# Hash attention and expert layers on one core: rounding the late heads' softmax planes straight from the exponentials

## The chip, the cores and the metric

The kernel runs on one core of a Trainium2 chip. A core has five engines that run side by side, each with an in-order queue of its own: TensorE (PE, matrix products; its weight loads are PEld), VectorE (DVE), ScalarE (ACT), GpSimd (POOL) and SyncE (SP), which issues most DMAs. They meet at semaphores. The metric is device time in microseconds (us), from the start of the program on the chip to its end; less is better.

## The reference

Four batches of eight heads, 768 positions, 64 columns. A position attends only to positions in its own hash bucket; a row without any partner gets a uniform softmax over all 768. The result of all heads is the input of a two-layer network with squared ReLU.

```python
q_bits = (np.einsum('bhsd,dk->bhsk', q, proj) > 0)      # 6 bits, k alike
mask = q_bucket[:, :, :, None] == k_bucket[:, :, None, :]
scores = scale * np.matmul(q, k.transpose(0, 1, 3, 2))
scores = np.where(mask, scores, -1000000000.0)
scores = scores - np.max(scores, axis=-1, keepdims=True)
attn = np.exp(scores)
attn = attn / (np.sum(attn, axis=-1, keepdims=True) + 1e-09)
x = np.matmul(attn, v)                  # then (3072 tokens) x 512
h = x @ w_in                            # 512 -> 2048
r = np.maximum(h, 0.0)
out = (s * (r * r) + b) @ w_out         # 2048 -> 512
```

## The kernel before

The program is written as steps (`plan.add`, `plan.any`), each with an engine or a choice of engines, an estimated cost, what it reads and writes, and a priority. `Plan.order` runs a small simulation with those costs and fixes the order of each engine's queue; where a step may run on several engines (`some`, `plan.any`), it takes the one that by the estimates is done first. On the chip the order is fixed; only the waits differ from the plan.

A slot is 256 rows of one head, two tiles of 128 rows; there are 32 x 3 = 96 slots. Heads 0 to 9 (slots 0 to 29) take the early way, in which the softmax is transposed by TensorE; `late(w)` is true for heads 10 to 31 (slots 30 to 95, 132 tiles), which write the softmax as two f16 planes and let a DMA transpose them.

The softmax of a slot is in `weights`. For each tile: two pairs of matmuls (L607, L608) make the scores, the hash mask among them, in a pair of PSUM banks (two pairs take turns); L612 (VectorE) takes the negated maximum into `st`; L613 (ScalarE) takes the exponential of scores plus that bias, with the row sum, into one of the five buffers of `eb`. For both tiles together, GpSimd marks rows without a partner from their maximum (L617 a huge addend for the sum, L618 the uniform value), and VectorE makes the inverse sum (L622, L623). Then GpSimd normalises each tile in place: exponential times inverse plus uniform value (L632). For late heads ScalarE rounds that times 2^15 to f16, the high plane (L639), VectorE makes the remainder, the low plane (L640), both into one of the two buffers of `pb`, and a DMA of SyncE transposes them into `tb` (L641). `values` multiplies the planes with the values (L678, L684 for late heads), `finish` moves the result to the network's input.

`st` holds for each slot of a ring of `NST` = 2 the maximum, the sum, its inverse and the two marks.

The expert layers (`moe`) need all heads of a batch. They have the lowest priority on TensorE and fill it between attention steps; a group of two 128-blocks has 24 matmuls of the first layer (L780 to L782) and 12 of the second (L807, with `ghb`, then with the remainder `glb`). Between the layers run L790 to L792 on ScalarE and L793, L794 on GpSimd. `decode` turns the experts' float64 weights into planes, on ScalarE, VectorE and GpSimd, during the first half.

Of the kernel before, what the change touches and what calls it, by code (L numbers as in the profile page):

```python
# [168 lines left out]
def lsh_attention_moe(ctx: ExitStack, tc, q, k, v, proj, w_in, w_out, s, b, out):  # L169
# [29 lines left out]
    def tile_(name, shape, dt=F32):  # L199
        return const.tile(shape, dt, name=name)  # L200
# [11 lines left out]
    def act(n, fn, r, w, pr, more=0.0, late_=0.0):  # L212
        plan.add(ACT, 0.21 + n / 1470.0 + more, fn, r, w, pr, late_)
# [74 lines left out]
    NST = 2  # L288
    misc = tile_("misc", [P, 8])
    st = tile_("st", [P, NST, 5, TPC])  # L290
# [44 lines left out]
    nc.vector.memset(zero, 0.0)  # L335
    nc.vector.memset(qk_sb[0:D], SCALE)
# [21 lines left out]
    def decode(u, pr):  # L358
# [23 lines left out]
        act(512, lambda: nc.scalar.activation(g, raw()[:, :, 1].bitcast(F32), AF.Copy, scale=float(2.0**-112)), rk + [("pace", u % PACE)], [gk], pr)  # L382
        act(512, lambda: nc.scalar.activation(words(0), raw()[:, :, 0].bitcast(U32), AF.Copy, scale=float(2.0**-29 * 0.9373)), [], rk, pr)
# [208 lines left out]
    def weights(i, pr):  # L592
# [4 lines left out]
        nm, z, rz, u, big_ = [st[:, y, m] for m in range(5)]  # L597
        nk, zk = [[("st", y, m, a) for a in range(TPC)] for m in range(2)]
        for a in range(TPC):
# [4 lines left out]
            for g in range(2):  # L604
# [11 lines left out]
        def missing():  # L616
            nc.gpsimd.tensor_scalar(big_, nm, -FLOOR, 1e30, ALU.is_gt, ALU.mult)  # L617
            nc.gpsimd.tensor_scalar(u, nm, -FLOOR, 1.0 / (S + EPS), ALU.is_gt, ALU.mult)  # L618
        pool(TPC, missing, nk, [("st", y, 3), ("st", y, 4)], pr, 0.7)
# [4 lines left out]
        dve(1, inverse, zk + [("st", y, 4)], [("st", y, 2)], pr, 0.32)  # L624
        for a in range(TPC):
            j = TPC * i + a
            e, ek = EB[ering(j)], EK[ering(j)]
            n, r = j % 2, tring(i)
            hi, lo, hk = pb[:, n, 0], pb[:, n, 1], EK[NE + n]

            def norm(eng, a=a, e=e):
                eng.tensor_scalar(e, e, rz[:, a:a + 1], u[:, a:a + 1], ALU.mult, ALU.add)  # L632
            ways = [(POOL, NORM, lambda norm=norm: norm(nc.gpsimd))]
            if not late(w) and not POOLN:
                ways.append((ACT, 0.93, lambda a=a, e=e: nc.scalar.activation(e, e, AF.Identity, bias=u[:, a:a + 1], scale=rz[:, a:a + 1])))
            plan.any(ways, [("st", y, 2), ("st", y, 3)], [ek], pr)
            if not late(w):
                continue
# [246 lines left out]
FIRST = 0.5  # L885
RATE = 1.0
# [11 lines left out]
POOLN = True  # L898
# [39 lines left out]
```

## Time and profile before

| | us |
|---|---|
| median of 3 runs | 966.34 (964.97 to 966.7) |
| profiled execution, its own time | 965.3 |
| its span, first to last instruction | 963.5 |
| TensorE busy in the span | 923.7 (96%) |
| VectorE, ScalarE, GpSimd busy | 600.3, 662.1, 589.5 |
| mean granted TensorE clock | 0.983 of full |

The durations used below come from the profiled execution. Busy time of an engine is the time covered by its instructions; a matmul's end is modelled, so TensorE's busy time alone does not say that it is at its peak. A wait is put down to the engine whose semaphore came last. An engine that is idle and not the bottleneck costs nothing.

### The profile page before, as it was taken

What the parts mean: (1) busy time and instruction counts of PE and PEld (TensorE: products, weight loads), DVE (VectorE), ACT (ScalarE), POOL (GpSimd) and SP (SyncE); (2) the same over time, 40 slices, a digit from 0 to 9 for tenths busy, and PEclk for the clock granted to TensorE, in tenths of its full rate; (3) what the DMA queues carried; (4) which work ended last, traced back from release to release, by engine and by line L of the source; (5) the groups of instructions that cost most, each with busy time, mean ns of one, the idle gap of its engine ahead of it and who ended that gap; (6) DMA issues with size and microseconds to landing.
All of it is one profiled execution on the core that took longest, in us unless ns stands there. A gap on an engine that the chain in (4) does not pass through costs nothing.

```text
span 963.5 us, 18096 instructions
## 1 busy us (share of the span) xinstructions
PE 923.7 (96%) x6512; PEld 732.1 (76%) x6512; DVE 600.3 (62%) x1020; ACT 662.1 (69%) x1235; POOL 589.5 (61%) x686
## 2 busy tenths in 40 slices
PE   8998779899999999999999999999999999999997
PEld 5876567677777777778787778877878888888886
DVE  6687887778788687676767677767667672000000
ACT  3787887888787667766677777777777775434342
POOL 2455654687598667566777666766767675433333
PEclk7999898999999999999999999999999999999999
DMA  4376675556898889997699798898897775101000
GB/s 116 93 191 197 181 197 161 142 158 154 219 200 179 188 199 200 206 202 155 141 191 183 163 205 170 165 200 162 177 188 152 170 132 105 55 9 37 12 22 22
DMA packets 303721, 144.44 MB, mean 150 GB/s; under 512 B 264256, under 2 KB 286784, under 8 KB 303632
## 3 DMA queue, kind: packets, MB, share of 16 engines
q1 hardware_dynamic: 298432, 126.25, 61.0%
q10 hardware_dynamic: 5200, 17.05, 5.9%
q8 instruction: 51, 0.84, 0.4%
q14 instruction: 38, 0.31, 0.1%
HBM read 51.38 MB, written 14.16 MB: 68 GB/s over the span
## 4 chain that ended last, share of the span: by engine, by line
PE 69%; DVE 9%; DMA 6%; POOL 6%; issue 5%; ACT 4%; POOLq 0%; SPq 0%; DVEq 0%; ACTq 0%
PE bank L807 21%; PE bank L780 7%; PE bank L782 7%; PE bank L781 7%; PE bank L607 6%; PE bank L608 5%; PE bank L678 4%; PE bank L672 3%; DVE st L612 3%; DMA tb<-pb 3%; PE bank L664 2%; PE bank L684 2%; POOL eb L632 2%; DMA vm<-in_v_dram 2%; PE bank L477 1%
## 5 line engine op out<-in xcount | busy, mean ns | idle before, releaser
L632 POOL TENSOR_SCALAR eb<-eb,st 128x768 f32<-128x768 f32 x176 | 201.0, 1147 | 57.3 <-DVE st L623 41.3
L807 PE MATMUL bank<-w,ghb 128*128 128x512 f32 x768 | 213.9, 407 | 0.0
L612 DVE TENSOR_REDUCE st<-bank 128x1 f32<-128x768 f32 x192 | 180.1, 951 | 54.0 <-PE bank L608 48.5
L780 PE MATMUL bank<-xc,wi 128*128 128x256 f16 x768 | 211.5, 275 | 0.0
L782 PE MATMUL bank<-xc,wi 128*128 128x256 f16 x768 | 209.3, 273 | 0.0
L781 PE MATMUL bank<-xc,wi 128*128 128x256 f16 x768 | 209.3, 273 | 0.0
L613 ACT ACTIVATE eb<-bank,st 128x768 f32<-128x768 f32 x176 | 157.4, 895 | 63.0 <-DVE st L612 29.8
L640 DVE SCALAR_TENSOR_TENSOR pb<-eb,pb 128x768 f16<-128x768 f32 x132 | 140.6, 1070 | 60.5 <-ACT pb L639 58.6
L793 POOL TENSOR_SCALAR rb<-rb,misc 128x512 f32<-128x512 f32 x96 | 79.8, 832 | 153.7 <-ACT ghb L792 137.8
L790 ACT ACTIVATE rb<-bank,dsc 128x512 f32<-128x512 f32 x95 | 65.3, 687 | 144.8 <-PE bank L782 137.4
L607 PE MATMUL bank<-ks,aq 128*128 128x384 f32 x384 | 147.2, 383 | 11.1 <-ACT eb L613 6.7
L807 PEld LDWEIGHTS bank<-w,ghb 128*128 128x128 f32 x768 | 135.4, 189 | 22.4 <-issue 1.0
L794 POOL TENSOR_TENSOR glb<-rb,ghb 128x512 fp32r<-128x512 f32 x96 | 132.7, 1383 | 5.8
L608 PE MATMUL bank<-ks,bq 76*128 76x384 f32 x384 | 132.7, 346 | 2.3 <-DMA bq<-nat 2.3
L639 ACT ACTIVATE pb<-eb 128x768 f16<-128x768 f32 x132 | 110.1, 837 | 22.5 <-DMA tb<-pb 20.6
L807 PE MATMUL bank<-w,glb 128*128 128x512 f32 x384 | 112.3, 401 | 1.3 <-POOL glb L794 1.3
L780 PEld LDWEIGHTS <-wi 128*128 128x128 f16 x768 | 74.9, 98 | 48.0 <-issue 41.5
L607 PEld LDWEIGHTS bank<-ks,aq 128*128 128x128 f32 x384 | 74.6, 194 | 29.1 <-ACT eb L613 10.6
L617 POOL TENSOR_SCALAR st<-st 128x2 f32<-128x2 f32 x96 | 43.3, 451 | 80.4 <-DVE st L612 68.0
L830 DVE COPY osb<-bank 128x256 f32<-128x256 f32 x4 | 1.5, 418 | 136.3 <-PE bank L807 135.7
L807 PEld LDWEIGHTS bank<-w,glb 128*128 128x128 f32 x384 | 70.2, 188 | 16.7 <-POOL glb L794 1.9
L782 PEld LDWEIGHTS <-wi 128*128 128x128 f16 x768 | 75.1, 98 | 8.6
(136 smaller groups left out, 1502.3 us busy)
## 6 DMA issues: line engine op xcount, KB each, us to landing
ks<-aq SPq DMA_DIRECT2D x60, 192.0 KB
raw<-in_moe_w_in_dram ACTq DMA_DIRECT2D x16, 512.0 KB
raw<-in_moe_w_out_dram ACTq DMA_DIRECT2D x16, 512.0 KB
xc<-xd SPq DMA_DIRECT2D x60, 128.0 KB
nat<-in_q_dram SPq DMA_DIRECT2D x32, 192.0 KB
nat<-in_k_dram SPq DMA_DIRECT2D x32, 192.0 KB
vm<-in_v_dram SPq DMA_DIRECT2D x32, 192.0 KB
xd<-xsb SPq DMA_DIRECT2D x48, 128.0 KB
```

The source lines that it names most:

```text
L607: nc.tensor.matmul(o, aq[:, ts], ks[0][:, cols], start=True, stop=False)
L608: nc.tensor.matmul(o, bq[0:HR, ts], ks[1][0:HR, cols], start=False, stop=True)
L612: dve(S, lambda a=a, sc=sc: nc.vector.tensor_reduce(nm[:, a:a + 1], sc, AX.XY, ALU.max, negate=True), bk, [nk[a]], pr, 0.88)
L613: act(S, lambda a=a, sc=sc, e=e: nc.scalar.activation(e.rearrange("p (g n) -> p g n", g=2), sc, AF.Exp, bias=nm[:, a:a + 1], accum_out=z[: ...
L632: eng.tensor_scalar(e, e, rz[:, a:a + 1], u[:, a:a + 1], ALU.mult, ALU.add)
L639: act(S, lambda e=e, hi=hi: nc.scalar.mul(hi, e, TOP), [ek], [hk], pr)
L640: dve(S, lambda e=e, hi=hi, lo=lo: nc.vector.scalar_tensor_tensor(lo, e, TOP, hi, ALU.mult, ALU.subtract), [ek, hk], [("lo", n)], pr, 1.0)
L780: nc.tensor.matmul(hp, w[:, 0, fs], xc[:, 0, :], start=(cc == 0), stop=False)
L781: nc.tensor.matmul(hp, w[:, 1, fs], xc[:, 0, :], start=False, stop=False)
L782: nc.tensor.matmul(hp, w[:, 0, fs], xc[:, 1, :], start=False, stop=(cc == NC_ - 1))
L794: pool(2 * CH, lambda r=r, gh=gh, gl=gl: nc.gpsimd.tensor_tensor(gl, r, f32(gh), ALU.subtract), [rk, hk], [lk], MP)
L807: nc.tensor.matmul(o, (gh, gh, gl)[z][:, ts], w[:, z % 2], start=(f == fa and z == 0), stop=(f == fz - 1 and z == 2))
```

## The change

For late heads the normalising pass is gone. The first rounding (high plane) multiplies the exponential by 2^15 over the sum, an operand read from memory for each row, on ScalarE or GpSimd (`HIWAYS`), and the remainder on VectorE does the same. A row without a partner is now treated in the exponential: one new VectorE instruction for each tile takes the maximum and the constant 1, each times "maximum small enough", as bias and scale of the exponential, so that both are 0 for such a row and each exponential is 1. The two marks on GpSimd are gone for late heads, and the inverse sum needs no addend. Early heads keep their steps. `st` becomes a ring of four with a column of ones, set once. The conversions of expert weights go through a helper that could choose an engine but is given only ScalarE (`CONV`).

```diff
-    NST = 2
+    NST = 4
-    st = tile_("st", [P, NST, 5, TPC])
+    st = tile_("st", [P, NST, 6, TPC])
...
+    nc.vector.memset(st[:, :, 1, :], 1.0)
...
-            act(S, lambda a=a, sc=sc, e=e: nc.scalar.activation(e.rearrange("p (g n) -> p g n", g=2), sc, AF.Exp, bias=nm[:, a:a + 1], accum_out=z[:, a:a + 1]),
-                bk + [nk[a]], [ek, zk[a]], pr, 0.15, 0.2)
...
+            if late(w):
+                dve(1, lambda a=a: nc.vector.scalar_tensor_tensor(st[:, y, 2:4, a], nm[:, a:a + 1].broadcast_to([P, 2]), -FLOOR, st[:, y, 0:2, a], ALU.is_le, ALU.mult), [nk[a]], [sk[a]], pr, 0.16)
+            act(S, lambda a=a, sc=sc, e=e: nc.scalar.activation(e.rearrange("p (g n) -> p g n", g=2), sc, AF.Exp, bias=st[:, y, 2, a:a + 1] if late(w) else nm[:, a:a + 1],
+                                                                scale=st[:, y, 3, a:a + 1] if late(w) else 1.0, accum_out=z[:, a:a + 1]), bk + [sk[a] if late(w) else nk[a]], [ek, zk[a]], pr, 0.15, 0.2)
+        rk = ("st", y, 5)
+        if not late(w):
...
+            return
 
         def inverse():
-            nc.vector.scalar_tensor_tensor(rz, z, EPS, big_, ALU.add, ALU.add)
+            nc.vector.tensor_scalar(rz, z, EPS, 1.0 / TOP, ALU.add, ALU.mult)
             nc.vector.reciprocal(rz, rz)
...
-            def norm(eng, a=a, e=e):
-                eng.tensor_scalar(e, e, rz[:, a:a + 1], u[:, a:a + 1], ALU.mult, ALU.add)
-            ways = [(POOL, NORM, lambda norm=norm: norm(nc.gpsimd))]
...
-            act(S, lambda e=e, hi=hi: nc.scalar.mul(hi, e, TOP), [ek], [hk], pr)
-            dve(S, lambda e=e, hi=hi, lo=lo: nc.vector.scalar_tensor_tensor(lo, e, TOP, hi, ALU.mult, ALU.subtract), [ek, hk], [("lo", n)], pr, 1.0)
+            some(S, lambda x, a=a, e=e, hi=hi: x.activation(hi, e, AF.Copy, scale=rz[:, a:a + 1]) if x is nc.scalar else x.tensor_scalar(hi, e, rz[:, a:a + 1], zero, ALU.mult, ALU.add), [ek, rk], [hk], pr, HIWAYS, NORM)
+            dve(S, lambda a=a, e=e, hi=hi, lo=lo: nc.vector.scalar_tensor_tensor(lo, e, rz[:, a:a + 1], hi, ALU.mult, ALU.subtract), [ek, hk, rk], [("lo", n)], pr, 1.0)
...
+CONV = (ACT,)
+CONVCOST = 0.95
...
-POOLN = True
+HIWAYS = (ACT, POOL)
```

## Rows read from the trace of the kernel before

**Rows 1.** By stretch: busy us (count) PE, PEld, DVE, ACT, POOL; clock; DMA share; GB/s.

```profile
0.00:240.00 240.00, 211.90 (x1634) 164.74 (x1634) 186.25 (x380) 183.58 (x398) 137.43 (x180) 0.94 0.59 160
240.00:320.00 80.00, 75.22 (x511) 58.04 (x510) 65.60 (x120) 62.91 (x116) 63.26 (x65) 1.00 0.89 196
320.00:805.00 485.00, 482.94 (x3355) 384.71 (x3354) 342.23 (x510) 350.78 (x628) 329.11 (x385) 1.00 0.87 176
805.00:963.00 158.00, 153.68 (x1019) 124.59 (x1016) 6.25 (x12) 64.78 (x96) 59.70 (x59) 1.00 0.11 32
```

**Rows 2.** Chain that ended last, at 341 and 866 us; start, us, what.

```profile
340.87 2.79 PE bank L807 x12
...
865.98 2.79 PE bank L807 x12
```

**Rows 3.** TensorE's waits from 240 to 320 us; total us, times, longest.

```profile
PE bank L678 <- DMA tb<-pb: 1.4, 1, 1.4
PE bank L607 <- ACT eb L613: 1.1, 2, 0.8
PE bank L477 <- DVE bq L480: 0.9, 1, 0.9
```

**Rows 4.** TensorE's waits from 320 to 810 us.

```profile
PE bank L607 <- DVE bq L480: 1.0, 2, 0.8
...
PE bank L607 <- ACT eb L613: 0.2, 1, 0.2
```

**Rows 5.** Waits of all engines from 320 to 810 us.

```profile
DVE pb L640 <- ACT pb L639: 52.1, 49, 3.6
...
ACT eb L613 <- DVE pb L640: 25.2, 21, 3.7
ACT pb L639 <- DMA tb<-pb: 17.0, 20, 1.8
...
ACT eb L613 <- DVE st L612: 6.9, 4, 2.3
```

**Rows 6.** Groups by line (busy us, mean ns, idle before); one line's durations min/median/max.

```profile
L632 POOL TENSOR_SCALAR eb<-eb,st 128x768 f32<-128x768 f32 x176 | 201.0, 1147 | 57.3 <-DVE st L623 41.3 <-ACT raw L383 4.3 <-ACT tb L228 4.1
L640 DVE SCALAR_TENSOR_TENSOR pb<-eb,pb 128x768 f16<-128x768 f32 x132 | 140.6, 1070 | 60.5 <-ACT pb L639 58.6 <-POOL xsb L733 1.3
L639 ACT ACTIVATE pb<-eb 128x768 f16<-128x768 f32 x132 | 110.1, 837 | 22.5 <-DMA tb<-pb 20.6 <-POOL eb L632 1.8
L791 ACT ACTIVATE rb<-rb 128x512 f32<-128x512 f32 x96 | 60.5, 630 | 1.8
L617 POOL TENSOR_SCALAR st<-st 128x2 f32<-128x2 f32 x96 | 43.3, 451 | 80.4 <-DVE st L612 68.0 <-DMA ks<-nat 4.7 <-PE bank L664 2.4
L622 DVE SCALAR_TENSOR_TENSOR st<-st 128x2 f32<-128x2 f32 x96 | 29.0, 302 | 28.4 <-ACT eb L613 14.2 <-POOL rb L793 6.0 <-POOL st L617 4.3
L419 ACT ACTIVATE wi<-raw,wsc 128x512 f16<-128x512 f32 x10 | 6.9, 722 | 0.4 <-DVE wsc L439 0.2
...
L622 DVE SCALAR_TENSOR_TENSOR st<-st x96: 143/160/1261, 22.7 to 795.6; 128x2 f32<-128x2 f32 x96
L640 DVE SCALAR_TENSOR_TENSOR pb<-eb,pb x132: 939/958/2043, 256.3 to 812.6; 128x768 f16<-128x768 f32 x132
```

**Rows 7.** In order of time, GpSimd and ScalarE at the first late tiles.

```profile
252.69 3.72 POOL L632 TENSOR_SCALAR eb<-eb,st 128x768 f32<-128x768 f32 x2 [0.32 <-DVE st L623]
...
255.47 0.84 ACT L639 ACTIVATE pb<-eb 128x768 f16<-128x768 f32 x1 [1.82 <-POOL eb L632]
```

**Rows 8.** The same in the middle of the late heads.

```profile
500.64 1.96 POOL L632 TENSOR_SCALAR eb<-eb,st 128x768 f32<-128x768 f32 x2 [0.56 <-DVE st L623]
...
512.05 0.84 ACT L639 ACTIVATE pb<-eb 128x768 f16<-128x768 f32 x1
...
520.77 0.84 ACT L639 ACTIVATE pb<-eb 128x768 f16<-128x768 f32 x1 [0.58 <-DMA tb<-pb]
```

**Rows 9.** Groups by line from 805 us to the end, TensorE.

```profile
L807 PE MATMUL bank<-w,glb 128*128 128x512 f32 x116 | 32.6, 396 | 1.3 <-POOL glb L794 1.3
```

More of the change, by code (lines that the diff above doesn't have):

```diff
@@ L381, in decode, with scaled, fn @@
             dve(1, lambda: nc.vector.tensor_reduce(wmx[:, j:j + 1], raw()[:, :, 1].bitcast(F32), AX.X, ALU.max, apply_absolute_value=True), rk, [("wx", j)], pr, 0.65)
-        act(512, lambda: nc.scalar.activation(g, raw()[:, :, 1].bitcast(F32), AF.Copy, scale=float(2.0**-112)), rk + [("pace", u % PACE)], [gk], pr)
-        act(512, lambda: nc.scalar.activation(words(0), raw()[:, :, 0].bitcast(U32), AF.Copy, scale=float(2.0**-29 * 0.9373)), [], rk, pr)
+        def scaled(out, src, by, r, w):
+            def fn(e):
+                if e is nc.scalar:
+                    e.activation(out(), src(), AF.Copy, scale=by)
+                else:
+                    e.tensor_scalar(out(), src(), by, 0.0, ALU.mult, ALU.add)
+            some(512, fn, r, w, pr, CONV, CONVCOST)
+        scaled(lambda: g, lambda: raw()[:, :, 1].bitcast(F32), float(2.0**-112), rk + [("pace", u % PACE)], [gk])
+        scaled(lambda: words(0), lambda: raw()[:, :, 0].bitcast(U32), float(2.0**-29 * 0.9373), [], rk)
         dve(512, lambda: nc.vector.scalar_tensor_tensor(words(0), gi, -2**31, words(0), ALU.bitwise_and, ALU.bitwise_or), [gk], rk, pr, 0.75)
@@ L596, in weights @@
         aq, bq, ks = AQ[x], BQ[x], KS[x]
-        nm, z, rz, u, big_ = [st[:, y, m] for m in range(5)]
-        nk, zk = [[("st", y, m, a) for a in range(TPC)] for m in range(2)]
+        nm, z, rz = [st[:, y, m] for m in (0, 4, 5)]
+        nk, sk, zk = [[("st", y, m, a) for a in range(TPC)] for m in (0, 2, 4)]
         for a in range(TPC):
@@ L612, in weights @@
             dve(S, lambda a=a, sc=sc: nc.vector.tensor_reduce(nm[:, a:a + 1], sc, AX.XY, ALU.max, negate=True), bk, [nk[a]], pr, 0.88)
-            act(S, lambda a=a, sc=sc, e=e: nc.scalar.activation(e.rearrange("p (g n) -> p g n", g=2), sc, AF.Exp, bias=nm[:, a:a + 1], accum_out=z[:, a:a + 1]),
-                bk + [nk[a]], [ek, zk[a]], pr, 0.15, 0.2)
-        def missing():
-            nc.gpsimd.tensor_scalar(big_, nm, -FLOOR, 1e30, ALU.is_gt, ALU.mult)
-            nc.gpsimd.tensor_scalar(u, nm, -FLOOR, 1.0 / (S + EPS), ALU.is_gt, ALU.mult)
@@ new lines, in weights, with missing, inverse @@
+        rk = ("st", y, 5)
+        if not late(w):
+            u, big_ = st[:, y, 2], st[:, y, 3]
+            def missing():
+                nc.gpsimd.tensor_scalar(big_, nm, -FLOOR, 1e30, ALU.is_gt, ALU.mult)
+                nc.gpsimd.tensor_scalar(u, nm, -FLOOR, 1.0 / (S + EPS), ALU.is_gt, ALU.mult)
+            pool(TPC, missing, nk, sk, pr, 0.7)
+            def inverse():
+                nc.vector.scalar_tensor_tensor(rz, z, EPS, big_, ALU.add, ALU.add)
+                nc.vector.reciprocal(rz, rz)
+            dve(1, inverse, zk + sk, [rk], pr, 0.32)
+            for a in range(TPC):
+                j = TPC * i + a
+                e, ek = EB[ering(j)], EK[ering(j)]
+                pool(S, lambda a=a, e=e: nc.gpsimd.tensor_scalar(e, e, rz[:, a:a + 1], u[:, a:a + 1], ALU.mult, ALU.add), [rk] + sk, [ek], pr, NORM)
+            return
@@ L621, in inverse @@
         def inverse():
-            nc.vector.scalar_tensor_tensor(rz, z, EPS, big_, ALU.add, ALU.add)
+            nc.vector.tensor_scalar(rz, z, EPS, 1.0 / TOP, ALU.add, ALU.mult)
             nc.vector.reciprocal(rz, rz)
-        dve(1, inverse, zk + [("st", y, 4)], [("st", y, 2)], pr, 0.32)
+        dve(1, inverse, zk, [rk], pr, 0.32)
         for a in range(TPC):
@@ L629, in weights @@
             hi, lo, hk = pb[:, n, 0], pb[:, n, 1], EK[NE + n]
-            def norm(eng, a=a, e=e):
-                eng.tensor_scalar(e, e, rz[:, a:a + 1], u[:, a:a + 1], ALU.mult, ALU.add)
-            ways = [(POOL, NORM, lambda norm=norm: norm(nc.gpsimd))]
[L634 to L638, printed above, removed]
-            act(S, lambda e=e, hi=hi: nc.scalar.mul(hi, e, TOP), [ek], [hk], pr)
-            dve(S, lambda e=e, hi=hi, lo=lo: nc.vector.scalar_tensor_tensor(lo, e, TOP, hi, ALU.mult, ALU.subtract), [ek, hk], [("lo", n)], pr, 1.0)
+            some(S, lambda x, a=a, e=e, hi=hi: x.activation(hi, e, AF.Copy, scale=rz[:, a:a + 1]) if x is nc.scalar else x.tensor_scalar(hi, e, rz[:, a:a + 1], zero, ALU.mult, ALU.add), [ek, rk], [hk], pr, HIWAYS, NORM)
+            dve(S, lambda a=a, e=e, hi=hi, lo=lo: nc.vector.scalar_tensor_tensor(lo, e, rz[:, a:a + 1], hi, ALU.mult, ALU.subtract), [ek, hk, rk], [("lo", n)], pr, 1.0)
             plan.add(SP, TCOST, lambda a=a, n=n, r=r: nc.sync.dma_start_transpose(tb[:, r, a].rearrange("p h t q -> p (h t) q"), pb[:, n].rearrange("p h n -> p (h n)")),
```

1 line of the change is left out of this document (removed).

## The prediction

> **What bounds the kernel now.** I read first the busy time by stretch [rows 1]. It cuts the run in four. Up to 240 us (heads 0 to 9, the early way) TensorE is busy 211.90 of 240 us; from 240 to 320 us, where the late heads start, 75.22 of 80; from 320 to 805 us (late heads and expert layers together) 482.94 of 485; behind 805 us only expert layers are left, and VectorE has all but stopped. A busy TensorE need not run at its peak, so I looked at the pace of one kind of matmul in the chain of waits: twelve of line 807 take 2.79 us at 341 us, in the middle of the late heads, and 2.79 us at 866 us, where nothing else competes [rows 2]. The busy time of the third stretch is thus work and not hidden waiting. What TensorE stands idle there is 485 - 482.9 = 2.1 us, in the second stretch 80 - 75.2 = 4.8 us: 6.9 us that a faster softmax could give back. The 28 us of the first stretch belong to early heads, whose arithmetic stays.
>
> The Trainium skill, page "Perfetto Trace Analysis", section "Identifying the Most-Contended Engine", tells the reader not to judge TensorE by its matmul busy share but by the share of its weight loads. By that rule 384.71 / 485 = 79% would leave a fifth of the stretch, some 100 us, to be won. The trace speaks against it here: in the last stretch, where TensorE waits for nothing, the same share is 124.59 / 158 = 79% [rows 1], so 79% is what this mix of matmuls loads when it is full.
>
> Next I read who waits for whom. In the second stretch TensorE's longest waits are 1.4 us for a transposing DMA into `tb` and 1.1 us for an exponential that frees a score bank [rows 3]. In the third they are 1.0 us and 0.2 us [rows 4]. In the third the other engines wait for one another: line 640 waits 52.1 us for line 639, exponentials wait 25.2 us for line 640 to free a buffer of `eb`, line 639 waits 17.0 us for the DMA to free a buffer of `pb` [rows 5]. That is a queue backed up from its far end.
>
> One slot shows how far. Its two normalising passes run at 500.64 us and are over at 502.6; the first rounding of the same tiles (line 639) starts at 512.05, nearly ten us later, and the next rounding into the same half of `pb` at 520.77, having waited for the DMA [rows 8]. One trip round that buffer is 520.77 - 512.05 = 8.7 us: rounding, remainder, DMA transposition. It sets the attention's pace; the normalising pass lies in front of it, in time that the tile spends waiting anyway.
>
> **The change part by part.** There are 66 late slots of two tiles: 132 tiles.
>
> Removed on GpSimd: 132 passes of line 632 at 1.147 us, 151 us, and in each of 66 slots line 617 at 0.451 us with its twin on the next line, at most 60 us [rows 6]. Where they lay: in steady state in the ten us above, so nothing there. At the start, where no `pb` buffer is taken, they are on the path: the first two late tiles are normalised at 252.69 us for 3.72 us, and ScalarE stood 1.82 us until the first was out [rows 7]; the exponential queued behind is the one that TensorE waits for. Without the pass those two waits should go: 1.1 us for the exponential and 1.4 us for the first transposes, which start up to 3.7 us sooner, together -2.5 us [rows 3]. Late next is then VectorE's preparation of the next head, 0.9 us in the same stretch, which stays.
>
> Added on VectorE: one instruction on 128x2 for each tile, between maximum and exponential: 132. No such row stands at this place; the nearest is line 622, the same operation and size: median 0.160 us, mean 0.302, worst 1.261. So 21 us by the median, 40 by the mean [rows 6]. I take the mean. It stands in VectorE's queue in front of whatever comes next and delays every exponential by 0.3 us. Its cover is ScalarE's own queue: in the third stretch ScalarE was idle for want of a maximum only 4 times, 6.9 us in all [rows 5]; 4 x 0.3 = 1.2 us of later exponentials, of which TensorE, which waited 0.2 us for them, should see next to nothing. If that cover goes, the price is up to 132 x 0.3 = 40 us on ScalarE, and TensorE sees what its two score banks don't hide.
>
> Pointer operands: on ScalarE a 512-wide pass with a scale read from memory takes 0.722 us (line 419) against 0.630 without (line 791), so +0.09 us for each exponential and each rounding that stays there [rows 6]: at most 132 x 2 x 0.09 = 24 us, about what a third of the roundings moved away (44 x 0.837 = 37 us) repays. For the remainder on VectorE no row isolates a pointer; I bound it between 0 and ScalarE's 0.09 us and take 0.09, 12 us. It can be less than nothing, because line 640 takes 1.070 us in the mean and 0.958 in the median [rows 6], and the long ones may owe their length to GpSimd, which loses work. VectorE's load in the third stretch, 342.23 of 485 us or 71% [rows 1], becomes at most (342 + 40 + 12) / 485 = 81%. The new reciprocal pair replaces one of equal count: nothing.
>
> Rounding on ScalarE or GpSimd, whichever the planner thinks is done first (0.73 against 1.1 us). On GpSimd the nearest row is the removed pass, same size: 1.147 us against 0.837 [rows 6]. This lies in the `pb` trip: +0.09 there on ScalarE, +0.31 on GpSimd, +0.09 for the remainder. So the trip gets 0.18 to 0.40 us longer, attention ends 66 x 0.18 = 12 to 66 x 0.40 = 26 us later. The cover is expert work already at hand: behind 805 us TensorE still has 116 / 4 = 29 groups of line 807 with `glb` [rows 9], 158 / 29 = 5.4 us each, of which 24 (three chunks of eight) belong to the last batch and wait for attention. Five groups, 27 us, are in stock. While that lasts a later end costs nothing; an earlier end gains nothing.
>
> The larger ring of `st` (4 for 2) frees columns that were reused after two slots, some 17 us, while a slot is done with them in about 10: nothing. One more memset at the start, and the conversions of the expert weights still have ScalarE as their only engine: nothing.
>
> **Sum.** The profiled execution took 965.3 us, 963.5 of it span and 1.8 around it. 965.3 - 2.5 = 962.8 us. It lies 1.0 us under the median of the runs shown, 966.34, so I forecast 963.8 us, 0.26% less.
>
> **The rivals.**
> *Hidden altogether.* The start-up gain is given back: the planner makes another order from 240 us on, and the first transposes still queue behind other DMAs (one DMA share of 0.89 there [rows 1]). For it: the waits are small and the order is new; against it: the 1.82 us of ScalarE's wait is a plain dependency that goes. About 966.3 us, within 0.2% (1.9 us, about what a measurement of this kernel can tell from no change). Chance 0.32.
> *A longer trip starves the end.* Rounding mostly on GpSimd, whose queue is in order: it now also waits for `pb`, and stands behind the expert remainders. The place is the trip of `pb`; it decides from 27 / 66 = 0.41 us more for each slot. With 0.31 + 0.09 and 0.1 us of queueing it is 0.5: (0.5 - 0.41) x 66 = 6 us, 965.3 + 6 + 1.0 = 972.3 us. For it: 0.40 is already the upper bound above; against it: the planner only takes GpSimd where it is thought quicker. Chance 0.20, with the smaller losses of a busier VectorE.
> *More than the start-up.* GpSimd loses a third of its work, long instructions on VectorE shrink, and all 6.9 us of TensorE's idle time go: 966.3 - 6.9 = 959.4 us. Against it: most of these waits are for head preparation and not for softmax. Chance 0.06.
> *The pass paces the run.* If TensorE were not full and the attention's trip set the end, a pass of 1.147 us less in each slot would take 66 x 1.147 = 76 us: 890 us. Against it: the ten us that a normalised tile waits [rows 8], and the 2.79 us of rows 2. Chance 0.02. (This is the case that the skill's rule on weight loads would allow.)
> *The change does not do what it says:* all roundings might stay on ScalarE. GpSimd is then simply freer, and the sum is the same.
>
> **How the numbers follow.** The forecast, a gain between 1.9 and about 5 us, has 0.40. Faster by over 0.2% is 0.40 + 0.06 + 0.02 = 0.48, within 0.2% 0.32, slower 0.20. The range runs from 958 (all idle time and a little of the pace) to 971.5 us (nearly the starved case). The forecast's own range is 961 to 964.4.
>
> **What would show it.** Right: TensorE still at 99% from 320 us on; the wait for the exponential and the first transposes gone between 240 and 320 us; the rounding's wait for the DMA unchanged or longer; the end of VectorE's work at 805 us or later. Wrong: VectorE over 85% busy with TensorE waiting for exponentials; TensorE's idle time behind the last head; GpSimd waiting for `pb`; or an attention that ends much sooner and a TensorE with fewer gaps before 240 us.

## The result and the profile after

| | before | after |
|---|---|---|
| median (9 runs each) | 967.13 us (964.97 to 968.84) | 972.1 us (969.48 to 975.99) |
| ratio of the times, 95% interval | 1 | 1.0061 (1.0045 to 1.0078) |
| profiled execution, its own time; its span | 965.3; 963.5 | 975.38; 973.5 |
| GpSimd busy in the span | 589.5 | 434.3 |

The change costs 0.6%, some 5 us. The forecast was a gain, and 972.1 lies outside its range. The profiled execution of after is one of its slowest, so its rows are read stretch by stretch and not by their sum.

Busy time of after by stretch, columns as in [rows 1]:

```profile
0.00:240.00 240.00, 211.11 (x1611) 164.08 (x1612) 183.03 (x377) 180.48 (x391) 134.02 (x178) 0.93 0.58 159
240.00:320.00 80.00, 76.12 (x499) 59.26 (x498) 70.87 (x130) 62.17 (x110) 46.93 (x41) 0.98 0.82 185
320.00:805.00 485.00, 479.97 (x3315) 382.75 (x3314) 367.52 (x624) 354.04 (x606) 189.63 (x183) 1.00 0.85 176
805.00:973.00 168.00, 163.66 (x1093) 132.75 (x1091) 8.46 (x14) 70.50 (x104) 63.72 (x62) 1.00 0.13 35
```

In the third stretch TensorE's idle time is now 485 - 479.97 = 5.0 us, in [rows 1] 2.1; VectorE went from 342.23 to 367.52 us, GpSimd from 329.11 to 189.63. Behind 805 us TensorE is as full as before (4.3 us idle in either), only with more left to do: it is busy for 163.66 us there, before for 153.68. So the time is lost while attention runs, not at its end.

TensorE's waits in the second and in the third stretch of after (total us, times, longest), to be held against [rows 3] and [rows 4]:

```profile
PE bank L616 <- DVE bq L489: 2.9, 2, 1.8
PE bank L486 <- DVE bq L489: 0.6, 1, 0.6
PE bank L616 <- DVE nat L507: 0.3, 1, 0.3
...
PE bank L616 <- ACT eb L624: 2.1, 4, 1.1
PE bank L616 <- DVE nat L507: 1.0, 2, 0.5
PE bank L503 <- ACT eb L624: 0.5, 1, 0.5
PE bank L616 <- DVE bq L489: 0.5, 2, 0.3
```

At the start-up the waits for the exponential and for the first transposed planes are gone, but VectorE's preparation of the next head (`bq`) has taken their place. From 320 us on, score matmuls wait 2.1 us for exponentials, in [rows 4] 0.2.

Other engines' waits of after from 320 to 805 us, against [rows 5]:

```profile
DVE pb L655 <- ACT pb L654: 24.5, 26, 2.2
...
ACT eb L624 <- DVE st L623: 22.9, 17, 2.4
...
POOL pb L654 <- DMA tb<-pb: 21.5, 8, 5.0
...
ACT eb L624 <- DVE pb L655: 16.2, 17, 3.4
...
ACT pb L654 <- DMA tb<-pb: 13.3, 14, 2.5
```

The exponential (L624) now waits 17 times, 22.9 us, for the new instruction (L623); for the maximum it had waited 4 times, 6.9 us. ScalarE's and VectorE's waits around `pb` got shorter. GpSimd, which now rounds too, has a new one: it waits 21.5 us for the DMA to free `pb`, which the prediction had named as a sign of being wrong. Which of these waits cost time, the first experiment shows.

Groups of after by line (busy us, mean ns of one):

```profile
L624 ACT ACTIVATE eb<-bank,st 128x768 f32<-128x768 f32 x176 | 169.7, 964 | 72.8 <-DVE st L623 31.3 <-DVE st L621 21.9 <-DVE pb L655 16.2
L655 DVE SCALAR_TENSOR_TENSOR pb<-eb,st,pb 128x768 f16<-128x768 f32 x132 | 140.5, 1072 | 38.1 <-ACT pb L654 33.0 <-POOL pb L654 4.7
L654 ACT ACTIVATE pb<-eb,st 128x768 f16<-128x768 f32 x109 | 99.4, 928 | 14.5 <-DMA tb<-pb 13.3 <-DVE st L647 1.1
L623 DVE SCALAR_TENSOR_TENSOR st<-st 128x2 f32<-128x2 f32 x132 | 37.6, 297 | 1.2
L654 POOL TENSOR_SCALAR pb<-eb,st,misc 128x768 f16<-128x768 f32 x23 | 24.2, 1052 | 47.1 <-DMA tb<-pb 23.8 <-DVE st L621 9.8 <-DVE st L623 6.2
```

The prices came close to the estimates: 0.297 us for the new instruction (0.302 put down), 0.928 for a rounding on ScalarE (0.837 before, +0.09 as put down), 1.052 for the 23 roundings that went to GpSimd (1.147 put down).

One measure carries the comparisons below: the starts of the first and the last of the 132 late maxima, from one row on their line. It leaves out what happens before 240 us, where the clock fell at other moments from one execution to the next. Instructions of that line in before, then in after: name, count, durations min/median/max ns, first and last start in us.

```profile
L612 DVE TENSOR_REDUCE st<-bank x132: 935/956/959, 237.3 to 790.4; 128x1 f32<-128x768 f32 x132
```

```profile
L621 DVE TENSOR_REDUCE st<-bank x132: 935/957/959, 240.8 to 798.7; 128x1 f32<-128x768 f32 x132
```

Before it is 790.4 - 237.3 = 553.1 us, after 798.7 - 240.8 = 557.9 us. I call it the length of late attention. Each kernel has one profiled execution, so this length has no interval of its own, and differences of some tenths of a us are not certain.

### The profile page after: what moved, and what is told of

Read it like the earlier page. It is cut to its first block, busy times and chain, and to the rows that moved or that the text cites. A ratio compares the mean times of both kernels' runs of the same rounds, so it can differ in the third digit from the quotient of the medians.

```text
span 973.5 us, 17871 instructions
## 1 busy us (share of the span) xinstructions
PE 930.9 (96%) x6512; PEld 738.8 (76%) x6512; DVE 629.9 (65%) x1142; ACT 667.2 (69%) x1209; POOL 434.3 (45%) x461
## 4 chain that ended last, share of the span: by engine, by line
PE 63%; DVE 14%; ACT 7%; issue 7%; POOL 5%; DMA 3%; SPq 0%; POOLq 0%; DVEq 0%; ACTq 0%
PE bank L822 19%; PE bank L795 6%; PE bank L797 6%; PE bank L796 6%; PE bank L616 6%; PE bank L617 5%; DVE st L621 4%; PE bank L693 3%; PE bank L687 3%; PE bank L679 3%; ACT eb L624 2%; DVE pb L655 2%; PE bank L699 2%; DMA bq<-nat 2%; PE bank L486 1%
## 5 line engine op out<-in xcount | busy, mean ns | idle before, releaser
L808 POOL TENSOR_SCALAR rb<-rb,misc 128x512 f32<-128x512 f32 x96 | 85.2, 887 | 302.9 <-ACT ghb L807 282.0
L624 ACT ACTIVATE eb<-bank,st 128x768 f32<-128x768 f32 x176 | 169.7, 964 | 72.8 <-DVE st L623 31.3
L655 DVE SCALAR_TENSOR_TENSOR pb<-eb,st,pb 128x768 f16<-128x768 f32 x132 | 140.5, 1072 | 38.1 <-ACT pb L654 33.0
L809 POOL TENSOR_TENSOR glb<-rb,ghb 128x512 fp32r<-128x512 f32 x96 | 136.8, 1425 | 7.4
L654 ACT ACTIVATE pb<-eb,st 128x768 f16<-128x768 f32 x109 | 99.4, 928 | 14.5 <-DMA tb<-pb 13.3
L795 PEld LDWEIGHTS <-wi 128*128 128x128 f16 x768 | 74.9, 97 | 42.5 <-issue 35.2
L797 PEld LDWEIGHTS <-wi 128*128 128x128 f16 x768 | 75.1, 98 | 8.5
L796 PEld LDWEIGHTS <-wi 128*128 128x128 f16 x768 | 75.6, 98 | 6.8
L807 ACT ACTIVATE ghb<-rb,misc 128x512 fp32r<-128x512 f32 x96 | 78.1, 814 | 2.1
```

What stands on the lines that cost most here:

```text
L654: some(S, lambda x, a=a, e=e, hi=hi: x.activation(hi, e, AF.Copy, scale=rz[:, a:a + 1]) if x is nc.scalar else x.tensor_scalar(hi, e, rz[: ...
L655: dve(S, lambda a=a, e=e, hi=hi, lo=lo: nc.vector.scalar_tensor_tensor(lo, e, rz[:, a:a + 1], hi, ALU.mult, ALU.subtract), [ek, hk, rk], [ ...
L795: nc.tensor.matmul(hp, w[:, 0, fs], xc[:, 0, :], start=(cc == 0), stop=False)
L796: nc.tensor.matmul(hp, w[:, 1, fs], xc[:, 0, :], start=False, stop=False)
L797: nc.tensor.matmul(hp, w[:, 0, fs], xc[:, 1, :], start=False, stop=(cc == NC_ - 1))
L808: pool(2 * CH, lambda r=r: nc.gpsimd.tensor_scalar(r, r, s_sb, b_sb, ALU.mult, ALU.add), [hk, "sb"], [rk], MP, 0.77)
```

## Experiments

There were two theories at first: that the new instruction and the second pointer make each exponential late (LATE), or that the new order and the roundings on GpSimd cost (ORDER). The edits below stand against after and are abridged.

### The same order without the new instruction (e5_cheap)

```diff
-dve(1, ... scalar_tensor_tensor(st[:, y, 2:4, a], nm[...].broadcast_to([P, 2]), -FLOOR, st[:, y, 0:2, a], is_le, mult) ...)
+dve(1, ... memset(st[:, y, 2:4, a], 1.0) ...)
-act(... bias=st[:, y, 2, a:a + 1] ..., scale=st[:, y, 3, a:a + 1] ...)
+act(... bias=nm[:, a:a + 1] ...)
```

> The changed kernel's order, instruction by instruction, but the new VectorE instruction is a memset of the same 128x2 (59 ns, no input), and the exponential has the maximum as its only pointer. Rows without a partner are not treated. LATE: 0.24 us and 0.08 us less in each tile give the loss back, 966 to 968.5 us, and TensorE's waits for exponentials behind 320 us fall under 0.7 us. ORDER: the order is the same, so 970 to 973 us with the same waits.

Measured: 964.46 us, ratio 0.9974 (0.9954 to 0.9995), still under the range of LATE. Every engine has the order of after; only the price of the new instruction and of the second pointer is gone. The late maxima take 787.6 - 237.4 = 550.2 us:

```profile
L621 DVE TENSOR_REDUCE st<-bank x132: 936/958/959, 237.4 to 787.6; 128x1 f32<-128x768 f32 x132
```

So in this order the folding of the normalisation into the roundings does bring 0.26%, about the -2.5 us of the forecast, and the treatment of rows without a partner (instruction and second pointer) costs 1.0061 - 0.9974 = 0.0087 of the time, 8.4 us. LATE stands, ORDER falls for this order.

The stretch from 320 to 805 us of e5_cheap, busy time and two of its waits, shows which waits cost nothing:

```profile
320.00:805.00 485.00, 483.00 (x3364) 388.85 (x3363) 351.04 (x624) 348.29 (x611) 196.44 (x184) 1.00 0.85 176
```

```profile
POOL pb L654 <- DMA tb<-pb: 32.4, 11, 5.2
...
ACT eb L624 <- DVE st L623: 18.7, 17, 3.5
```

GpSimd waits longer for `pb` than in after, and exponentials wait 17 times for the memset, as often as for the new instruction; yet this kernel is the faster one. What sets the two apart is TensorE: it is idle for 485 - 483.00 = 2.0 us in this stretch, in after for 5.0, and its waits for exponentials are 0.6 us in place of 2.1.

### Three more, each in an order of its own

Without the new instruction, the planner free (e2_fold):

```diff
-            if late(w):
-                dve(1, ... scalar_tensor_tensor(...) ...)
-... bias=st[:, y, 2, a:a + 1] if late(w) else nm[:, a:a + 1], scale=st[:, y, 3, a:a + 1] if late(w) else 1.0
+... bias=nm[:, a:a + 1]
```

> The fold alone: no normalising pass, rounding straight from the exponentials with the inverse sum, but the exponential as before, with the maximum as its only pointer operand and no new VectorE instruction. Rows without a partner are not treated, which leaves that part of the result out. Theory LATE (TensorE waits because the new instruction of 0.30 us and the second pointer, 0.08 us, make each exponential free its score bank 0.4 us later): the loss goes, 965 to 968 us, and TensorE's waits for exponentials behind 320 us fall from 2.1 us to under 0.5. Theory ORDER (the planner wrote another order, in which GpSimd waits for transposes): 970 to 974 us, GpSimd still waiting 15 us or more for the DMA.

Measured: 968.43 us, 1.0009 (0.9991 to 1.0027), between the two ranges: no loss, and no gain either.

With the new instruction, but the normalising pass kept on GpSimd (e3_small):

```diff
+            pool(S, ... gpsimd.tensor_scalar(e, e, rz[:, a:a + 1], zero, mult, add) ...)
+            act(S, ... scalar.mul(hi, e, TOP) ...)
-            some(S, ... scale=rz[:, a:a + 1] ..., HIWAYS, NORM)
```

> The new instruction alone: bias and scale of the exponential made on VectorE, but the normalising pass stays on GpSimd (without the uniform value) and both roundings are as before. LATE: the whole loss stands here too, 970 to 974 us, with TensorE's waits for exponentials at 2 us or more behind 320 us. ORDER: no rounding on GpSimd and no wait for a transpose there, so 965 to 968.5 us.

Measured: 978.81 us, 1.0111 (1.0081 to 1.0141), above both expectations.

All roundings on ScalarE (e4_act):

```diff
-HIWAYS = (ACT, POOL)
+HIWAYS = (ACT,)
```

> The changed kernel with ScalarE as the only engine for the first rounding. LATE: still 970 to 974 us, perhaps a little more, since ScalarE does 23 more passes of 0.93 us. ORDER, in the form that GpSimd's waits for the transposing DMA (23.8 us in 9 waits) hold up the expert remainders: 965 to 968.5 us.

Measured: 976.87 us, 1.0092 (1.0057 to 1.0127), again above both ranges: slower than after, not faster. These three change the planner's order as well, and the last two lose more than any part of the change weighs alone. They say that an order can cost as much as the change; they can't price a part. From here on, but for e12_aside, the order was kept, or changed alone.

### The second pointer alone (e6_ptr), the instruction alone (e7_stt)

Both in the order of after. The first is e5_cheap with a scale pointer to the 1.0; the second has the real instruction and one pointer:

```diff
 e6_ptr:  memset as in e5_cheap
+         bias=nm[:, a:a + 1], scale=st[:, y, 3, a:a + 1]
 e7_stt:  scalar_tensor_tensor as in after
+         bias=st[:, y, 2, a:a + 1], scale=1.0
```

> The changed kernel in its own order, but the new VectorE operation is a memset to 1.0 (59 ns in the run with the memset and one pointer), and the late exponential takes the maximum as its bias and that 1.0 as its scale, so it keeps two pointers (rows without a partner are not treated: that part of the computation is left out). Against the run with one pointer (964.5 us) only the second pointer is put back, which in the traces makes one exponential 0.98 us in place of 0.90. Theory POINTER (the 132 longer exponentials carry the loss of 7.6 us, being last of the chain scores, maximum, exponential, weight load): 970 to 972.5 us. Theory OPERATION (the extra two-input instruction between maximum and exponential, 0.30 us on average, carries it): 964.5 to 966.5 us. If both count by their length alone, 0.08 of the 0.32 us that the chain gained: about 966.4 us.

> The changed kernel in its own order with the new VectorE operation as it is and its first result as the bias of the exponential, but the scale is the constant 1.0, so the exponential has one pointer (rows without a partner are not treated: that part of the computation is left out). The counterpart of the run with the second pointer alone. Theory OPERATION: 969.5 to 972 us, nearly the whole loss, with TensorE's waits for the exponential as in the changed kernel (2.1 us in the middle stretch). Theory POINTER: 964.5 to 967 us. By length alone, 0.24 of 0.32 us: about 970.2 us. If this and the run with the second pointer do not add up to the 7.6 us, the two lengthen the chain past a point from which it costs, and neither does alone.

Measured: e6_ptr 964.88 us, 0.9997 (0.9982 to 1.0012); e7_stt 968.13 us, 1.0048 (1.0026 to 1.0069). Late maxima, e6_ptr and then e7_stt:

```profile
L621 DVE TENSOR_REDUCE st<-bank x132: 937/956/959, 239.6 to 790.2; 128x1 f32<-128x768 f32 x132
```

```profile
L621 DVE TENSOR_REDUCE st<-bank x132: 935/957/960, 236.2 to 790.9; 128x1 f32<-128x768 f32 x132
```

550.6 us with the second pointer, 554.7 with the instruction, against 550.2 with neither. The pointer is worth 0.4 us here, the instruction 4.5: OPERATION, not POINTER. By the ratios to before it is 0.0023, with intervals that overlap, and 0.0074, which is clear of them. In microseconds e7_stt lies between the ranges of its two theories; the kernel before, measured beside it, was faster too (965.36 us, beside e5_cheap 967.25).

### Is it the length of the instruction, or the times in which it is held up? (e8_two, e10_const)

The durations of the new instruction in after are far apart:

```profile
L623 DVE SCALAR_TENSOR_TENSOR st<-st x132: 140/156/1257, 243.9 to 800.0; 128x2 f32<-128x2 f32 x132
```

Its median is 0.156 us, its mean 0.297, so about 132 x (0.297 - 0.156) = 18.6 us are time in which it was held up. (The 37.6 us of its group count overlapping instructions once.) By the timeline of after, 71 of the 132 run with no GpSimd instruction beside them and take 0.140 to 0.163 us. Of the 61 others 28 are short too, and 33 take over 0.2 us; each of these 33 ends within 0.03 us of the end of a GpSimd instruction. One such case, GpSimd's and then VectorE's row (start us, duration us):

```profile
536.49 1.29 POOL L809 TENSOR_TENSOR glb<-rb,ghb 128x512 fp32r<-128x512 f32 x1
```

```profile
536.54 1.25 DVE L623 SCALAR_TENSOR_TENSOR st<-st 128x2 f32<-128x2 f32 x1
```

It starts 0.05 us behind a GpSimd instruction that reads two tensors, and ends with it (537.79 and 537.78 us). Two forms with other inputs, both in the order of after and with the whole computation:

```diff
 e8_two:
+ tensor_scalar(st[:, y, 2, a], nm[:, a], misc[:, 6] (= 1e9), nm[:, a], is_le, mult)
+ tensor_scalar(st[:, y, 3, a], nm[:, a], -FLOOR, 1.0, is_le, mult)
 e10_const:
+ tensor_scalar(st[:, y, 2, a], nm[:, a], 40.0, None, min)
+ tensor_scalar(st[:, y, 3, a], nm[:, a], -FLOOR, 1.0, is_le, mult)
```

> The changed kernel with the new operation written as two VectorE instructions that each read one column through a single tensor input, the floor test and the product by their two scalars; the computation is whole. In the trace of the changed kernel the one two-input instruction takes 0.15 us where GpSimd is idle and up to 1.26 us beside GpSimd's work. Theory HELD UP (the loss comes from the cases in which GpSimd's work holds the instruction up, not from its own length): the two would together take about 0.2 us and hardly ever more than 0.4, and the time is 966.5 to 969 us. Theory LENGTH (an instruction more in the chain costs whatever its form, and VectorE's queue ahead of it does the rest): 971.5 to 975 us, since two take more than one.

> The changed kernel in its own order on every engine, its computation whole, with the new operation written as two VectorE instructions of one column that take one tensor input and constants alone: the smaller of 40 and the negated maximum, which stays finite where a row has no partner, and the 1 or 0 of the floor test. In the run with two instructions of one column, the one with constants alone took 142 ns on average beside 265 ns for the one that also read its two scalars from memory. The two should so take 0.28 to 0.30 us, as much as the one instruction of the changed kernel on average (0.30 us), but with no long cases. Theory HELD UP (the loss comes from the cases of 0.8 to 1.26 us): 966 to 969 us. Theory LENGTH (it comes from the mean time that stands between maximum and exponential): 970 to 973 us.

The second instruction pair needs no product: with a scale of 0 a row without a partner becomes uniform for any finite bias, and the smaller of 40 and the negated maximum is finite.

Measured: e8_two 970.28 us, 1.0056 (1.0036 to 1.0076); e10_const 966.39 us, 0.9991 (0.9975 to 1.0007). Their new instructions, e8_two and then e10_const:

```profile
L624 DVE TENSOR_SCALAR st<-st,misc x132: 252/265/275, 244.8 to 797.2; 128x1 f32<-128x1 f32 x132
...
L625 DVE TENSOR_SCALAR st<-st x132: 132/143/149, 245.0 to 797.3; 128x1 f32<-128x1 f32 x132
```

```profile
L623 DVE TENSOR_SCALAR st<-st x132: 132/145/155, 241.5 to 791.4; 128x1 f32<-128x1 f32 x132
...
L624 DVE TENSOR_SCALAR st<-st x132: 135/144/148, 241.5 to 791.4; 128x1 f32<-128x1 f32 x132
```

None of these 528 is ever held up: the longest takes 0.275 us. In e10_const the time is back at that of before, in the range of HELD UP. But its pair is not as long as its expectation had it: the second instruction starts 0.06 us behind the start of the first, and from the start of the first to the end of the second it is 0.207 us (mean of 132), where the one instruction of after takes 0.297. The time of e10_const alone can't tell HELD UP from LENGTH. The pair of e8_two can: it takes 0.326 us from start to end, longer than the instruction of after, and has no long cases. Busy time from 320 to 805 us of e7_stt, e8_two and e10_const:

```profile
320.00:805.00 485.00, 480.66 (x3337) 384.83 (x3334) 366.93 (x622) 344.00 (x604) 191.26 (x183) 1.00 0.85 175
```

```profile
320.00:805.00 485.00, 482.63 (x3343) 386.31 (x3342) 376.92 (x742) 357.46 (x610) 191.01 (x184) 1.00 0.87 178
```

```profile
320.00:805.00 485.00, 482.83 (x3354) 386.49 (x3353) 366.19 (x738) 356.74 (x607) 193.51 (x183) 1.00 0.87 176
```

TensorE is idle for 4.3 us in e7_stt, whose instruction is held up, and for 2.4 and 2.2 us with the two pairs, which are not; in after it was 5.0, in e5_cheap 2.0. VectorE is busiest in e8_two (376.92 us, in after 367.52), and yet TensorE waits less than in after. So in this stretch HELD UP holds, as far as one execution of each can show. One piece of e10_const shows both forms beside GpSimd's work, VectorE's rows first:

```profile
250.39 0.15 DVE L623 TENSOR_SCALAR st<-st 128x1 f32<-128x1 f32 x1
250.46 0.14 DVE L624 TENSOR_SCALAR st<-st 128x1 f32<-128x1 f32 x1
250.69 1.63 DVE L577 SCALAR_TENSOR_TENSOR vb<-vn,vsc,vb 128x384 f16<-128x384 f32 x1
```

```profile
249.99 0.67 POOL L576 TENSOR_SCALAR vb<-vn,vsc,misc 128x384 f16<-128x384 f32 x1
250.62 1.29 POOL L811 TENSOR_TENSOR glb<-rb,ghb 128x512 fp32r<-128x512 f32 x1
```

The new pair runs at its usual 0.15 us beside GpSimd's L576, which reads one tensor; the two-tensor instruction behind it (L577, 0.857 us in the mean of 22) starts beside L811, which reads two, and takes 1.63 us. Beside L811 the new form is not held up either: 52 of the 264 instructions of e10_const run beside it, and none takes more than 0.155 us. The Trainium skill, page "SBUF — State Buffer", section "Who interferes with whom", states it as a rule: a VectorE instruction with two SBUF inputs contends with a GpSimd instruction that reads SBUF, over ports that one of them holds exclusively; one with at most one input (outside the two-port modes) does not contend. The rows agree: 1.257 us at most for the one form, 0.275 for the other.

The time of e8_two seems to speak against it: 970.28 us lies between its two ranges, and its ratio is near that of after though nothing is held up. Its late maxima and those of e10_const:

```profile
L621 DVE TENSOR_REDUCE st<-bank x132: 937/956/959, 241.7 to 795.8; 128x1 f32<-128x768 f32 x132
```

```profile
L620 DVE TENSOR_REDUCE st<-bank x132: 939/957/959, 238.3 to 790.0; 128x1 f32<-128x768 f32 x132
```

554.1 and 551.7 us. Part of the difference is TensorE's clock. In after and in e8_two it fell between 275 and 285 us, in e10_const it didn't; busy time by stretch, 260 to 275 and 275 to 285 us, of after, e8_two and e10_const:

```profile
260.00:275.00 15.00, 15.00 (x103) 12.14 (x102) 13.70 (x38) 12.15 (x21) 12.10 (x10) 1.00 0.86 176
275.00:285.00 10.00, 8.10 (x45) 6.08 (x44) 9.54 (x15) 7.22 (x13) 7.26 (x8) 0.83 1.05 218
```

```profile
260.00:275.00 15.00, 14.95 (x102) 12.03 (x101) 13.86 (x40) 11.86 (x22) 10.93 (x9) 1.00 0.94 212
275.00:285.00 10.00, 8.27 (x45) 6.84 (x44) 9.13 (x19) 7.56 (x14) 8.84 (x6) 0.83 0.80 199
```

```profile
260.00:275.00 15.00, 13.25 (x94) 10.39 (x92) 14.44 (x39) 11.77 (x21) 13.83 (x12) 1.00 0.76 171
275.00:285.00 10.00, 9.88 (x66) 7.82 (x67) 8.98 (x21) 8.25 (x15) 8.03 (x6) 1.00 1.11 247
```

A mean of 0.83 is a third of the ten us at 1.2 in place of 2.4 GHz; TensorE had been busy 15.00 and 14.95 of the 15 us ahead of it, 13.25 where it did not fall. It costs about 10 x (1 - 0.83) = 1.7 us. A TensorE without gaps doesn't by itself bring the fall: in before and in e2_fold it was busy for 15.00 us of the same 15 and the clock stayed at 1.00, in e4_act for 13.08 and the clock fell to 0.83. Why it fell where it did stays open. The first 240 us differ too, at an order that is the same: their mean clock is 0.91 in e8_two, 0.94 in e10_const. Three of the six executions of e8_two have a mean clock of 0.977 or 0.978 and take 971.1 to 972.7 us. The other three, at 0.982 to 0.986, take 966.7 to 969.4 us; at such clocks after takes 969.5 to 972.7 and e10_const 965.9 to 969.7. Three are few: the total time of e8_two doesn't settle the question, and what speaks for HELD UP is the stretch above, in one execution of each kernel.

With the 1.7 us taken off where the clock fell in that place, the late maxima of all runs in the order of after read:

| run | new instruction or pair: mean us; longest instruction | pointers | TensorE idle, 320 to 805 us | late maxima, us |
|---|---|---|---|---|
| e5_cheap | 0.060; 0.060 | 1 | 2.0 | 550.2 |
| e6_ptr | 0.060; 0.060 | 2 | 2.4 | 550.6 |
| e10_const | 0.207; 0.155 | 2 | 2.2 | 551.7 |
| e8_two | 0.326; 0.275 | 2 | 2.4 | 554.1 - 1.7 = 552.4 |
| e7_stt | 0.292; 1.257 | 1 | 4.3 | 554.7 |
| after | 0.297; 1.257 | 2 | 5.0 | 557.9 - 1.7 = 556.2 |

Length alone costs 1.1 us for 0.15 us more in each tile (e6_ptr to e10_const) and 0.7 for another 0.12 (to e8_two). Being held up costs 556.2 - 552.4 = 3.8 us against a pair that takes longer in the mean. That is the main part; LENGTH is not nothing.

### Does it matter where the instruction stands? (e12_aside, e13_lo)

```diff
 e12_aside: scalar_tensor_tensor as in after, but
-  exponential waits for it, bias=st[:, y, 2, a:a + 1], scale=st[:, y, 3, a:a + 1]
+  exponential waits for the maximum, bias=nm[:, a:a + 1]
 e13_lo:    e5_cheap, and in the step of the remainder
+  scalar_tensor_tensor(st[:, y, 2:4, a], nm[...].broadcast_to([P, 2]), -FLOOR, st[:, y, 0:2, a], is_le, mult)
   scalar_tensor_tensor(lo, e, rz[:, a:a + 1], hi, mult, subtract)
```

> The changed kernel with the new operation still issued on VectorE behind each late maximum, but nobody reads its results: the exponential waits for the maximum alone and takes it as its only pointer (rows without a partner are not treated: that part of the computation is left out; the planner lays out the order anew). Theory OCCUPANCY (the 132 instructions cost because they push back what follows them on VectorE, the next maximum and the lo roundings): 968 to 971 us, as the run in which the exponential waits for the operation and has one pointer (968.1). Theory WAIT (they cost because they stand between maximum and exponential): 964 to 966.5 us, as the run with the memset (964.5).

> The kernel with the memset in place of the new operation and one pointer (964.5 us, 0.9974 of before; rows without a partner are not treated: that part of the computation is left out), with the two-input instruction of the changed kernel put back 132 times in another place: on VectorE just ahead of each rounding of the remainders (lo), its result read by nobody. The order on every engine is that of the changed kernel. It takes VectorE's time (132 instructions, by the trace of after 0.30 us on average and up to 1.26 us) but does not stand between a maximum and its own exponential. Theory OCCUPANCY (held-up instructions cost wherever they stand, since the next maximum waits behind them): 968.5 to 972 us. Theory PLACE (they cost only between maximum and exponential): 964 to 966.5 us.

Measured: e12_aside 980.01 us, 1.0132 (1.0116 to 1.0147), above both expectations. The planner had drawn up another order, in which 37 roundings went to GpSimd; it decides nothing. e13_lo keeps the order: 970.78 us, 1.0047 (1.0027 to 1.0067). Its added instruction and its late maxima:

```profile
L656 DVE SCALAR_TENSOR_TENSOR st<-st x132: 140/154/1237, 257.0 to 815.9; 128x2 f32<-128x2 f32 x132
```

```profile
L621 DVE TENSOR_REDUCE st<-bank x132: 936/957/959, 240.6 to 796.3; 128x1 f32<-128x768 f32 x132
```

796.3 - 240.6 = 555.7 us; in this run, too, the clock fell near 280 us (0.91 in the mean from 270 to 290), so about 554.0, against 550.2 without the instruction and 554.7 with it between maximum and exponential. OCCUPANCY, not PLACE: it costs nearly as much where its own exponential does not wait for it. That points to VectorE's queue as the place where the time is lost. TensorE is idle for 485 - 481.18 = 3.8 us from 320 to 805 us. That VectorE's queue alone does it is not shown: the instruction now stands in front of the remainder, in the trip of `pb`, and no run puts it where nothing but VectorE's queue is behind it.

### The planner's prices, alone and with the cheaper form (e9_price, e11_both)

```diff
 e9_price, new instruction and late exponential:
-  ..., 0.16)      -  ..., 0.15, 0.2)
+  ..., 0.36)      +  ..., 0.23 if late(w) else 0.15, 0.2)
 e11_both: e9_price with the two instructions of e10_const
```

> The changed kernel, its computation whole, with the planner told the prices of the trace of after: 0.36 us in place of 0.16 for the new operation and 0.08 us more for a late exponential with two pointers. The planner then lays out another order. Theory PLANNER (the chain is late because the order was drawn up with too low a price, so that score products and maxima are issued too late for their weight loads): 966 to 969.5 us, and TensorE's waits for the exponential between 320 and 805 us fall from 2.1 to under 1 us. Theory CHAIN (the longer chain runs in a ring of four buffers whose length no order can shorten, so its price stays): 971 to 974 us.

> The computation whole: the two instructions with constants alone, as in the run beside this one, in the order that the planner draws up when it is told the measured prices (the same order on every engine as the run with these prices alone, 966.4 us, 1.0016 of the kernel before). Theory HELD UP: 963 to 965.5 us, faster than both kernels. Theory LENGTH: 966 to 968 us, as the run with the prices alone.

Measured: e9_price 966.41 us, 1.0016 (0.9999 to 1.0033); e11_both 965.8 us, 0.9998 (0.9979 to 1.0017). The order drawn up with the measured prices wins back most of the loss, though it keeps the two-tensor form. There the form is held up less: its mean is 0.242 us, and 21 of the 132 take over 0.2 us, in after 33. Whether the prices did it or this order merely suits, one order can't tell. TensorE's waits for exponentials in the middle stretch fall as expected, to

```profile
PE bank L486 <- ACT eb L624: 0.4, 1, 0.4
```

e11_both misses the gain that HELD UP expected (963 to 965.5 us): both remedies together are no better than one, and against e9_price it can't be told apart. No complete version beats before.

## Why the prediction was wrong, step by step

*Bound.* Right: TensorE is at 479.97 / 485 = 99% from 320 to 805 us in after, and behind 805 us it is idle for 4.3 of 168 us. In a kernel so full the time follows small delays of the engines that feed it.

*Start-up gain, -2.5 us.* The step failed. The two waits of [rows 3] did go, but "late next is then VectorE's preparation of the next head, 0.9 us in the same stretch, which stays" was wrong. Before, TensorE waited for `bq` in two places, the second of them this:

```profile
PE bank L607 <- DVE bq L480: 0.6, 1, 0.6
```

These 0.9 + 0.6 us grew to 2.9 + 0.6, and TensorE's idle time in the stretch only fell from 4.8 us to 80 - 76.12 = 3.9. In e5_cheap it is 80 - 75.31 = 4.7 us, as before: there the waits that went have made room for one of 1.9 us for `bq` and one of 1.6 us behind the memset:

```profile
PE bank L616 <- DVE bq L489: 1.9, 1, 1.9
PE bank L616 <- DVE st L623: 1.6, 1, 1.6
```

That the fold is worth 0.26% all the same (e5_cheap) agrees with the sum by its size, not by its place, and so by luck. Where its 2.5 us lie, no run isolates.

*The new instruction.* Its price was right: 132 x 0.297 = 39 us where 40 were put down. Its cover was not. "TensorE [...] should see next to nothing" is the step that failed, and the one that decides: the instruction and its pointer cost 8.4 us (e5_cheap to after), and TensorE's idle time from 320 to 805 us went from 2.0 to 5.0. The cover was counted in the order of before, as the four times in which ScalarE had waited for a maximum [rows 5]. In the order of after exponentials wait behind their maximum 17 times even where the instruction is a memset, so that cover was gone with the order itself. And the step asked only what the exponential loses, not what else stands in VectorE's queue: in e13_lo the instruction costs nearly as much where its exponential does not wait for it. The rows of before had what was needed: line 622 with 0.160 us in the median and 1.261 at worst [rows 6]. The prediction took the mean and spread it evenly; what costs is the tail.

*Pointers.* The size was right and so was the verdict. An exponential with two pointers instead of one: means 964 ns in after and, in e7_stt, 896 over the same 176, so (964 - 896) x 176 / 132 = 91 ns for a late one, as put down; a rounding 928 - 837 = 91 ns. The remainder's median went from 958 to 1018 ns in after, 0.06 us where 0.09 was put down, and its mean hardly moved (1.070 to 1.072 us). All of the exponential's part costs 0.4 us of late attention (e6_ptr), by the ratios 0.0023 and not clear of noise.

*The trip of `pb`, and the rival that starved the end.* That rival's time, 972.3 us, is what came out, by chance: the cause is another. GpSimd does wait for `pb` now, 21.5 us, and ScalarE's wait became shorter (13.3 us for 17.0), 34.8 us together. But in e5_cheap GpSimd waits 32.4 us and nothing is lost, matmuls wait for transposed planes no longer than before, and behind 805 us TensorE is idle for 4.3 us in both. The stock of expert work covered the later end, as the prediction said. VectorE's load came to 367.52 / 485 = 76%, under the 81% that it allowed; no share of busy time would have shown the loss.

*"More than the start-up".* Its thought that VectorE's long instructions shrink when GpSimd loses a third of its work came half true. The remainder's mean stood 1.070 - 0.958 = 0.112 us over its median before and stands 1.072 - 1.018 = 0.054 us over it after, 132 x 0.058 = 7.7 us less. But what GpSimd kept was enough to hold up 33 of the 132 new ones, for some 18.6 us.

*The other rivals.* "Hidden altogether" is what e2_fold shows, the fold alone in an order of its own (1.0009), but not what the whole change did. That the pass paces the run is refuted: GpSimd is busy for 155 us less, and no run gains more than 0.26%.

*Still open.* The late maxima explain 556.2 - 550.2 = 6.0 of the 8.4 us between e5_cheap and after. The rest has the size of what the clock does before 240 us, at one and the same order there: its mean is 0.93 in after, 0.94 in e5_cheap, 0.91 to 0.96 in all, and 0.01 of 240 us is 2.4 us. Whether the change has a part in that was not settled. Nor was it why e3_small, e4_act and e12_aside, in orders of their own, lose up to 13 us.

## What to carry to other kernels

On VectorE a small instruction in front of a chain is priced by its inputs and not only by its size: with two tensor inputs it can be held up while GpSimd works, with one input and constants it was not, and here two of the second kind beat one of the first. Where the planner's price is a median (0.16) and the mean is 0.30, try the mean, or take a form without the tail. Instructions of one engine may overlap: take the length of a pair from its first start to its last end, not from the sum of its parts. When a bound engine is 99% busy, look for the cover of an added step in every queue that it enters, and in the order that the change will have: "the engine behind it seldom waits" says nothing of the waits that it will make.

## What the runs showed of the hardware

- A scalar_tensor_tensor on 128x2 takes 0.140 to 0.163 us with no GpSimd instruction beside it and up to 1.257 us beside one, with whose end it then ends; a tensor_scalar on 128x1 with constants stays within 0.155 us beside the same work.
- Scalars read from memory make a tensor_scalar on 128x1 slower, but never held up: 0.265 us with two of them, 0.145 with constants.
- TensorE's mean clock from 275 to 285 us was 0.83 in after, e8_two, e13_lo and e4_act and 1.00 in the others. The 15 us ahead were without a gap in the first three (15.00, 14.95 and 15.00 busy), but in e4_act they were not (13.08), and in before and e2_fold they were (15.00 each) and the clock stayed. The spans of after's runs go with their mean clock: 967.6 us at 0.986, 974.1 at 0.977.
